# Late chunks transposed by DMA, five chunks loaded ahead of the first weights, and blocks of two chunks first, in a fused retention and FFN kernel

## The chip, the cores and the metric

One core of one Trainium2 chip. The metric is the device time of one execution in microseconds (us), the median of several runs; executions of one kernel mostly lie within 0.5% of their median. "Span" is the time between the first and the last instruction of the profiled execution; here a run is about 2 us longer than its span. A run counts as slow when it is over 1.5% above the fastest of its kernel; comparisons use fast runs.

## The reference

A linear attention with decay ("retention") over 4 batches, 8 heads, 768 steps and 64 dimensions, then an FFN with a squared ReLU over the 3072 tokens.

```python
for t in range(S):                                   # S = 768, per batch and head
    state = gamma * state + outer(k[t], v[t])
    y[t] = scale * q[t] @ state
x = y.transpose(0, 2, 1, 3).reshape(3072, 512)
out = square(relu(x @ w_in)) @ w_out                 # w_in 512 x 2048, w_out 2048 x 512
```

## The kernel before

The 3072 tokens are 24 chunks of 128. A chunk is loaded (q, k, v, 256 KB each), cast to bf16, q and k are transposed, one "visit" on TensorE does its attention (from the middle of the kernel on, one visit joins the end of a chunk's attention with the scores of the next), and its 128 rows `xt` go through FFN1 (by blocks of chunks) and FFN2 (by chunk).

The kernel does not write its instructions one after another. It records operations with their dependences and estimated durations, and a list scheduler in the kernel (`Plan`) simulates them and fixes the order on every engine before anything runs:

```python
def schedule(self, nbanks, max_open):
    ...
    while done < n:                       # the operation that can start first, by its estimates
        ...
                    key = (t, o["prio"], i)
                    if best is None or key < best[0]:
                        best = (key, i, eng)
        ...
            if move:                      # a DMA: charged to the shared DMA engines
                dur, n_desc = (dur[:2] if t < 50 else dur[:1] * 2), dur[2]
                eng_free[eng] = t + 0.08
                for w in range(2):
                    shared[w] = max(shared[w], t + self.DMA_LATENCY) + dur[w]
                end[i] = max(shared) + self.LAND
        ...
    return sorted(range(n), key=lambda i: (start[i], i))

SMALL = (1.20, 1.55, 65)                  # a 256 KB load: us of DMA, us of DMA, descriptors
PAIR = (1.4, 1.6, 9)
WIDE = (2.75, 2.75, 33)                   # a weight part, 1 MB
STORE = (0.72, 0.72, 9)
BLOCKS = [1, 1, 2, 2, 2, 4, 4, 4, 4]      # chunks per FFN1 block
ORDER = "p0 i0 i1 p1 i2 i3 o0 o1 o2 p2 o3"   # p: two chunks, i: w_in part, o: w_out part
```

From chunk 6 on the transposes are 32 small matmuls (from chunk 7 on inside the visit). They write the same PSUM tile `yy` that the visit uses, and ScalarE evicts them:

```python
def flips(m):
    ...
                    for a in range(2):
                        nc.tensor.transpose(tpv[...], bf[name][m % NBF][r, j, a, :], ident[r, r])   # 64x64

def evacuate(m):
    pl.add(f"E{m}", "ACT", 1.0, ("yy0", "yy1"), qkeys(m), ...)

def visit(m, n, t=None):                  # values and state of chunk m, scores and sums of n, transposes of t
    ...
```

## Time and profile before

| | |
|---|---|
| time | 226.85 us median of 3 runs (226.68 to 227.45) |
| span | 225.5 us |
| TensorE busy | 204.8 us (91%) |
| FFN matmuls alone, dense | 166 us: 192 groups of four 512-column matmuls at 0.865 us, read from the chain of waits |

The first lines are the groups of the page of before: source line, engine, operation, output<-inputs, shapes, count, then busy us and mean ns of one, then the idle time of the engine just before such instructions and what ended most of it.

```profile
L593 PE MATMUL fps<-xt,w_in 128*128 128x512 bf16 (+2 forms) x566 | 93.7, 309 | 3.9 <-POOL w_in L345 2.0
L631 PE MATMUL fps<-w_out,h 128*128 128x512 bf16 x368 | 90.1, 379 | 1.7 <-issue 1.3
...
L555 DVE TENSOR_TENSOR xt<-yy,yf 128x512 bf16<-128x512 f32 x24 | 16.6, 690 | 21.6 <-ACT qkT L436 18.1
L436 ACT ACTIVATE qkT<-yy 128x1024 bf16<-128x1024 bf16 x18 | 18.4, 1023 | 18.2 <-PE yy L468 17.5
```

L593 is FFN1 and L631 FFN2. The record lacks 26 of their 960 matmuls. The xt multiplication waits 18.1 us in all for the eviction of the transposes, which reads the same tile `yy`.

One piece of the chain of waits of before (start us, us, what) shows the cost of the transposes:

```profile
89.30 0.38 PE yy L389 x32
...
90.32 1.03 ACT qkT L436
...
91.37 0.70 DVE xt L555
...
92.12 1.89 PE fps L593 x8
```

The 32 small transposes take 0.38 us of TensorE, and FFN1 of a new block waits for their eviction and then for xt.

### The profile page before, as it was taken

How to read it: one execution, taken by the hardware profiler on the slowest of the kernel's cores; microseconds unless marked ns; L12 is line 12 of the kernel's file. 1: busy time of each engine (PE TensorE's matmuls, PEld its weight loads, DVE VectorE, ACT ScalarE, POOL GpSimd, SP SyncE). 2: the span in 40 equal slices, each digit the busy share in tenths (PEclk: the TensorE clock that was granted, in tenths of full speed). 3: DMA queues.
4: the chain of work that ended last, by engine and by line, in shares of the span. 5: the costliest groups of instructions: out<-in, count | busy, mean ns of one | idle time of the engine just before them, and what ended most of it. 6: DMA issues, size and time to landing. Idle time of an engine off the chain costs nothing.

```text
span 225.5 us, 7244 instructions
## 1 busy us (share of the span) xinstructions
PE 204.8 (91%) x3210; PEld 116.0 (51%) x3236; DVE 112.7 (50%) x250; ACT 106.0 (47%) x168; POOL 39.0 (17%) x65
## 2 busy tenths in 40 slices
PE   4786778699999999999989999999999999999993
PEld 1545667554577875455545554444444444444441
DVE  1583955873188786699957765432222222220000
ACT  8315635644357552677555555434335444343121
POOL 3213224224323322332242200000000000000000
PEclk9997999999999999999999999999999999999999
DMA  6999999999999999998988510110011110111212
GB/s 150 265 337 189 337 376 237 184 346 197 283 211 200 236 187 213 231 202 179 206 188 177 146 49 3 47 49 12 35 47 47 49 47 1 47 49 47 93 49 91
DMA packets 70975, 34.02 MB, mean 151 GB/s; under 512 B 63008, under 2 KB 63008, under 8 KB 70944
## 3 DMA queue, kind: packets, MB, share of 16 engines
q1 hardware_dynamic: 70944, 33.56, 58.8%
q8 instruction: 25, 0.41, 0.8%
q14 instruction: 6, 0.05, 0.1%
HBM read 27.26 MB, written 6.29 MB: 149 GB/s over the span
## 4 chain that ended last, share of the span: by engine, by line
PE 75%; SPq 11%; DMA 7%; issue 2%; ACT 2%; DVE 1%; POOL 0%; ACTq 0%; POOLq 0%
PE fps L631 34%; PE fps L593 32%; DMA qn<-in_q_dram 7%; SPq L569 6%; SPq L362 4%; PE yy L389 3%; PE yy L468 2%; SPq L356 2%; PE yy L453 1%; ACT qkT L436 1%; PE sc L479 1%; PE sc L490 1%; DVE xt L555 1%; POOL qs L345 0%; PE yy L402 0%
## 5 line engine op out<-in xcount | busy, mean ns | idle before, releaser
L593 PE MATMUL fps<-xt,w_in 128*128 128x512 bf16 (+2 forms) x566 | 93.7, 309 | 3.9 <-POOL w_in L345 2.0
L631 PE MATMUL fps<-w_out,h 128*128 128x512 bf16 x368 | 90.1, 379 | 1.7 <-issue 1.3
L598 ACT ACTIVATE h<-fps 128x512 bf16<-128x512 f32 x96 | 56.6, 596 | 52.6 <-PE fps L593 51.5
L593 PEld LDWEIGHTS <-w_in 128*128 128x128 bf16 x576 | 50.5, 99 | 35.4 <-issue 2.1
L603 DVE TENSOR_TENSOR h<-h 128x512 bf16<-128x512 bf16 x96 | 42.4, 456 | 49.7 <-ACT h L598 49.5
L631 PEld LDWEIGHTS <-h 128*128 128x128 bf16 x384 | 36.7, 98 | 42.9
L555 DVE TENSOR_TENSOR xt<-yy,yf 128x512 bf16<-128x512 f32 x24 | 16.6, 690 | 21.6 <-ACT qkT L436 18.1
L436 ACT ACTIVATE qkT<-yy 128x1024 bf16<-128x1024 bf16 x18 | 18.4, 1023 | 18.2 <-PE yy L468 17.5
L639 ACT ACTIVATE osb<-fps 128x512 f32<-128x512 f32 x24 | 14.3, 597 | 21.7 <-PE fps L631 21.4
L377 DVE TENSOR_TENSOR vs<-vn,vf 128x512 bf16<-128x512 f32 x24 | 17.6, 735 | 4.8 <-DMA vn<-in_v_dram 4.8
L345 POOL CAST ks<-kn 128x512 bf16<-128x512 f32 x20 | 13.5, 677 | 35.0 <-DMA kn<-in_k_dram 19.8
L345 POOL CAST qs<-qn 128x512 bf16<-128x512 f32 x21 | 14.7, 701 | 27.3 <-DMA qn<-in_q_dram 27.3
L546 DVE TENSOR_TENSOR state<-sc,state 128x256 bf16<-128x256 f32 x40 | 16.7, 419 | 0.5
L533 DVE TENSOR_TENSOR pt<-sc,cmask 128x512 bf16<-128x512 f32 x24 | 16.3, 681 | 0.0
L468 PE MATMUL yy<-qkT,state 64*64 64x64 bf16 x352 | 12.5, 198 | 1.0 <-issue 0.6
L453 PE MATMUL yy<-pt,vs 64*64 64x64 bf16 x384 | 7.8, 195 | 2.8 <-DVE pt L533 1.4
L468 PEld LDWEIGHTS <-state 64*64 64x64 bf16 x352 | 7.6, 105 | 2.0 <-PE yy L468 1.1
L453 PEld LDWEIGHTS <-vs 64*64 64x64 bf16 x384 | 5.3, 107 | 5.5 <-issue 2.9
L479 PE MATMUL sc<-qkT 64*64 64x64 bf16 x384 | 7.9, 196 | 0.1
L341 ACT ACTIVATE w_in<-wst 128x512 bf16<-128x512 f32 x7 | 4.1, 623 | 7.7 <-DMA wst<-in_moe_w_in_dram 7.6
L490 PE MATMUL sc<-vs,ks 64*64 64x64 bf16 x352 | 7.6, 196 | 0.0
L693 PE MATMUL fps<-ident 128*128 128x512 bf16 x12 | 5.8, 605 | 1.6 <-POOL ident L297 1.6
(45 smaller groups left out, 85.0 us busy)
## 6 DMA issues: line engine op xcount, KB each, us to landing
vn<-in_v_dram SPq DMA_DIRECT2D x24, 256.0 KB, 5.9
out_dram<-osb SPq DMA_DIRECT2D x24, 256.0 KB, 2.0
kn<-in_k_dram SPq DMA_DIRECT2D x18, 256.0 KB, 5.5
qn<-in_q_dram SPq DMA_DIRECT2D x18, 256.0 KB, 5.7
wst<-in_moe_w_in_dram SPq DMA_DIRECT2D x4, 1024.0 KB, 9.7
wst<-in_moe_w_out_dram SPq DMA_DIRECT2D x4, 1024.0 KB, 10.5
kn<-in_k_dram SPq DMA_DIRECT2D x3, 512.0 KB, 11.6
qn<-in_q_dram SPq DMA_DIRECT2D x3, 512.0 KB, 13.4
```

The costliest lines, as they stand in the source:

```text
L345: nc.gpsimd.tensor_copy(o, t)
L377: lambda: nc.vector.tensor_tensor(out=o[:], in0=t.rearrange("s (h d) -> s h d", h=H), in1=vf[:, i, :, None].to_broadcast([P, H, D]), op=AL ...
L436: lambda: nc.scalar.activation(qkT.rearrange("p x j (s t) -> p s (x j) t", s=2), tpv.rearrange("p s (g t) -> p s g t", t=L), AF.Copy), pri ...
L453: nc.tensor.matmul(yy[L * c : L * c + L, sub, p * L : p * L + L], lhsT=vs[r, 4 * a + j, :], rhs=pt[r, a, j, :], start=(p == 0), stop=True, ...
L468: nc.tensor.matmul(yy[L * c : L * c + L, sub, p * L : p * L + L], lhsT=st[r, j, :], rhs=qkT[r, 1, j, sub * L : sub * L + L], start=False, ...
L533: lambda: nc.vector.tensor_tensor(out=pt[:], in0=sc[:, :, 0:256].rearrange("s g (p t) -> s g p t", p=NJ), in1=cmask[:, None, None, :].to_b ...
L546: f = lambda cc=cc, j1=j1, j0=j0: nc.vector.tensor_tensor(out=sts[j1][:], in0=cc, in1=sts[j0][:], op=ALU.add)
L555: lambda: nc.vector.tensor_tensor(out=xt[:, :, u * C : u * C + C].rearrange("s p (g t) -> s g p t", g=2), in0=yy[:, :, 0:256].rearrange("s ...
L593: nc.tensor.matmul(ps[:, u * n : u * n + n], lhsT=w_in_bf[j][:, cb, c * P : (c + 1) * P], rhs=xt[:, cb, cols], start=(cb == 0), stop=(cb = ...
L598: nc.scalar.activation(h2[:, f0 : f0 + per, cols], ps[:].rearrange("p (u n) -> p u n", u=per), AF.Relu)
L603: nc.vector.tensor_mul(hv, hv, hv)
L631: nc.tensor.matmul(ps[:], lhsT=h2[:, fb, u * C : u * C + C], rhs=w_out_bf[j][:, c, :], start=(fb == 0), stop=(fb == NFB - 1))
```

## The change

The intent: take the late transposes off TensorE and ScalarE and give them to the DMA queue; load five chunks before the first weights, with neighbours in the queue from different chunks because the scheduler is told that this makes a load cheaper (0.95 us, not 1.20 to 1.55); begin with blocks of two chunks; and store the last chunk in two halves.

```diff
-SMALL = (1.20, 1.55, 65)
-PAIR = (1.4, 1.6, 9)
+SMALL = (0.95, 0.98, 65)          # neighbour from another chunk
+CLASH = (1.20, 1.55, 65)          # neighbour from the same chunk
+TURN = (1.05, 1.05, 9, 1.2)       # DMA transpose; the 4th number: us that it holds its queue
-BLOCKS = [1, 1, 2, 2, 2, 4, 4, 4, 4]
-SPLIT = 6
+BLOCKS = [2, 2, 2, 2, 4, 4, 4, 4]
+SPLIT = 8
+AHEAD = 4
-LEAD = 7
-NFP = 3
-F2LAG = 5.0
+LEAD = 5
+NPE = 7
+F2LAG = 6.0
-ORDER = "p0 i0 i1 p1 i2 i3 o0 o1 o2 p2 o3"
+ORDER = ("q0 q1 k0 k1 o0 v0 v1 q2 q3 k2 o1 q4 v2 k3 k4 k5 v3 o2 i0 i1 v4 q5 i2 i3 v5 q6 v6 o3 k6 k7 v7 q7")
 ...
     def transpose(m):
-        pl.add(f"T{m}", "PE", 0.45, ..., lambda: flips(m), ...)      # 32 of 64x64
-        evacuate(m)
+        if m >= NPE:
+            pl.add(f"X{m}", "SP", TURN, (bfk, bfq), qkeys(m),
+                   lambda: nc.sync.dma_start_transpose(out=..., in_=...), prio=-0.5)
+            return
+        for x, name in enumerate("kq"):                              # 4 of 128x128 each, evicted by ACT or DVE
 ...
+            parts = 2 if q4 == NM - 1 else 1                         # the last chunk's output in halves
```

(Cut: the buffers, the removed paired loads, the plumbing of `AHEAD`, and a change of the scheduler itself: it now charges every DMA with holding its queue, 0.6 us unless a fourth number says otherwise, where it charged 0.08. The comments and the shortened arguments are mine.)

More of the change, by code (lines that the diff above doesn't have):

```diff
@@ L38, in __init__, with add @@
         self.readers = {}
-    def add(self, name, eng, dur, reads=(), writes=(), fn=None, prio=0.0, lat=0.0, bank=None, after=(), count=0):
+    def add(self, name, eng, dur, reads=(), writes=(), fn=None, prio=0.0, lat=0.0, bank=None, after=(), count=0, tag=None):
         i = len(self.ops)
@@ L60, in add @@
         self.ops.append(dict(i=i, name=name, eng=eng, flex=flex, deps=sorted(deps), fn=fn,
-                             prio=prio, lat=lat, bank=bank, count=count))
+                             prio=prio, lat=lat, bank=bank, count=count, tag=tag))
         return i
@@ L87, in schedule @@
         outstanding = {e: [] for e in eng_free}
+        recent = []
         done = 0
@@ L121, in schedule @@
                     t = max(t, out_.pop(0)[0])
+                hold = dur[3] if len(dur) > 3 else 0.6
             start[i] = t
@@ L130, in schedule @@
             if move:
-                dur, n_desc = (dur[:2] if t < 50 else dur[:1] * 2), dur[2]
-                eng_free[eng] = t + 0.08
+                n_desc = dur[2]
+                if dur is SMALL:
+                    if recent[-1:] == [o["tag"]]:
+                        dur = CLASH
+                recent.append(o["tag"])
+                dur = dur[:2] if t < 50 else dur[:1] * 2
+                eng_free[eng] = t + hold
                 for w in range(2):
@@ L136, in schedule @@
                 out_.append((max(shared), n_desc))
-                dur = 0.08
+                dur = hold
             else:
@@ L194 @@
 WPRIO = {"in": -2.0, "out": 2.0}
-ORDER = "p0 i0 i1 p1 i2 i3 o0 o1 o2 p2 o3"
+ORDER = (
+    "q0 q1 k0 k1 o0 v0 v1 q2 q3 k2 o1 q4 v2 k3 k4 k5 v3 o2 i0 i1 v4 q5 i2 i3 v5 q6 v6 o3 k6 k7 v7 q7"
+)
 def dma_order(nm):
-    seq = []
-    for t in ORDER.split() + [f"c{m}" for m in range(nm)]:
-        n = int(t[1:])
-        if t[0] == "p":
-            new = [("k", 2 * n), ("q", 2 * n), ("v", 2 * n), ("v", 2 * n + 1)]
-        else:
-            new = [(x, n) for x in "kqv"] if t[0] == "c" else [("in" if t[0] == "i" else "out", n)]
-        seq += [x for x in new if x not in seq]
-    return seq
+    names = {"i": "in", "o": "out"}
+    seq = [(names.get(t[0], t[0]), int(t[1:])) for t in ORDER.split()]
+    return seq + [(x, m) for m in range(nm) for x in "kqv" if (x, m) not in seq]
 @with_exitstack
@@ L246 @@
         assert 512 % (n * C) == 0 and x // 4 == (x + n - 1) // 4
-    NLD, NBF, NQT, NXT, NH2, NWS, NOSB, NST = 4, 4, 4, 4, 3, 4, 3, 6
+    NLD, NBF, NQT, NXT, NH2, NWS, NOSB, NST = 4, 5, 5, 4, 3, 4, 3, 6
     NBANK = 4
@@ L265 @@
     ld = {x: sb(f"{x}n", [P, NLD, H * D], FP32) for x in "qkv"}
-    bf = {x: [sb(f"{x}s{j}", [P, NJ, 2, D] if x != "v" else [P, H, D], BF16) for j in range(NBF)] for x in "qkv"}
+    kq = [sb(f"kqs{j}", [P, 2, NJ, 2, D], BF16) for j in range(NBF)]
+    bf = {"k": [t[:, 0] for t in kq], "q": [t[:, 1] for t in kq]}
+    bf["v"] = [sb(f"vs{j}", [P, H, D], BF16) for j in range(NBF)]
     qkts = [sb(f"qkT{j}", [P, 2, NJ, P], BF16) for j in range(NQT)]
@@ L278 @@
     yy = psum.tile([P, 2, 512], FP32, name="yy")
-    tpv = yy[:, :, 256:512].bitcast(BF16)
     fps = [psum.tile([P, 512], FP32, name=f"fps{j}") for j in range(NBANK)]
@@ L352, in prepare @@
             t = ld[x][:, slot, :]
-            if x != "v" and m < 2 * NFP:
-                if m % 2 == 0:
-                    pl.add(f"ld{x}{m}", "SP", PAIR, (), (f"ld{x}{slot}", f"ld{x}{slot + 1}"),
-                           lambda x=x: nc.sync.dma_start(
-                               ld[x][:, slot : slot + 2, :].rearrange("s u n -> s (u n)"),
-                               src[x][b, :, i * C : (i + 2) * C, :].rearrange("h (w t) d -> w h (t d)", t=16)),
-                           prio=dma_prio[(x, m)])
-                continue
             pl.add(f"ld{x}{m}", "SP", SMALL, (), (f"ld{x}{slot}",),
@@ L364, in prepare @@
                        src[x][b, :, i * C : (i + 1) * C, :].rearrange("h s d -> s h d")),
-                   prio=dma_prio[(x, m)])
+                   prio=dma_prio[(x, m)], tag=m)
         for x in "kq":
             t, o = ld[x][:, slot, :], bf[x][m % NBF]
-            if m < 2 * NFP:
-                pl.add(f"c{x}{m}", CAST[x], 0, (f"ld{x}{slot}",), (f"bf{x}{m % NBF}",),
-                       lambda on, t=t, o=o: copy_on(on, o.rearrange("s j a d -> s (j a d)"), t), prio=urgency(m))
-                continue
             pl.add(f"c{x}{m}", CAST[x], 0, (f"ld{x}{slot}",), (f"bf{x}{m % NBF}",),
@@ L380, in prepare @@
                prio=urgency(m))
-    def flips(m):
-        for x, name in enumerate("kq"):
-            for j in range(NJ):
-                for sub in range(2):
-                    r = slice(L * sub, L * sub + L)
-                    for a in range(2):
-                        nc.tensor.transpose(tpv[L * a : L * a + L, sub, 256 * x + j * L : 256 * x + j * L + L],
-                                            bf[name][m % NBF][r, j, a, :], ident[r, r])
-    def flip_rows(m, x):
-        to, key = (sc, "sc") if x == "k" else (yy, "yy")
-        for u in range(2):
-            bt = bf[x][(m + u) % NBF].rearrange("s j a d -> s (j a d)")
-            def fn(u=u, bt=bt):
-                for t in range(8):
-                    for a in range(2):
-                        nc.tensor.matmul(to[L * a : L * a + L, u, L * t : L * t + L], lhsT=bt[:, t * D : t * D + D],
-                                         rhs=ident.rearrange("p (w h) -> p w h", h=H)[:, :, NJ * a : NJ * a + NJ],
-                                         start=True, stop=True, skip_group_check=True)
-            pl.add(f"T{x}{m}.{u}", "PE", 0.35, (f"bf{x}{(m + u) % NBF}", "ident"), (f"{key}{u}",), fn,
-                   prio=-200 + m, lat=0.2, count=16)
-        cols = to.rearrange("p s n -> p (s n)").rearrange("p (t u w j) -> p u j w t", u=2, j=NJ, w=8)
-        for u in range(2):
-            o = qkts[(m + u) % NQT][:, "kq".index(x)].rearrange("p j (w t) -> p j w t", t=16)
-            pl.add(f"E{x}{m + u}", EVAC, 0, (f"{key}0", f"{key}1"), (f"qkT{(m + u) % NQT}.{x}",),
-                   lambda on, u=u, o=o: copy_on(on, o, cols[:, u]), prio=urgency(m + u), lat=0.05)
@@ L413, in natural_keys @@
-    def natural_keys(m):
-        qkT, ks = qkts[m % NQT], bf["k"][m % NBF]
-        o1 = {}
-        def back():
-            ps = fps[o1["op"]["bank_index"]].bitcast(BF16)
-            for j in range(NJ):
-                nc.tensor.transpose(ps[:, j * P : j * P + P], qkT[:, 0, j, :], ident[:])
-        i0 = pl.add(f"B{m}", "PE", 0.24, (qkeys(m)[0], "ident"), (f"gB{m}",), back, prio=-200 + m, lat=0.2, count=4,
-                    bank=("open", ("B", m), False))
-        o1["op"] = pl.ops[i0]
-        pl.add(f"G{m}", EVAC, 0, (f"gB{m}",), (f"bfk{m % NBF}",),
-               lambda on: copy_on(on, ks.rearrange("s j a d -> s (j a d)"),
-                                  fps[o1["op"]["bank_index"]].bitcast(BF16)[:, 0:512]),
-               prio=urgency(m), bank=("close", ("B", m)))
@@ L430, in qkeys, with fn @@
     def qkeys(m):
         return [f"qkT{m % NQT}.{x}" for x in "kq"]
-    def evacuate(m):
-        qkT = qkts[m % NQT]
-        pl.add(f"E{m}", "ACT", 1.0, ("yy0", "yy1"), qkeys(m),
-               lambda: nc.scalar.activation(
-                   qkT.rearrange("p x j (s t) -> p s (x j) t", s=2),
-                   tpv.rearrange("p s (g t) -> p s g t", t=L), AF.Copy), prio=urgency(m), lat=0.05)
-    def transpose(m):
-        pl.add(f"T{m}", "PE", 0.45, (f"bfk{m % NBF}", f"bfq{m % NBF}", "ident"), ("yy0", "yy1"),
-               lambda: flips(m), prio=-200 + m, lat=0.2, count=32)
-        evacuate(m)
+    def transpose(m):
+        qkT, t = qkts[m % NQT], kq[m % NBF]
+        if m >= NPE:
+            pl.add(f"X{m}", "SP", TURN, (f"bfk{m % NBF}", f"bfq{m % NBF}"), qkeys(m),
+                   lambda: nc.sync.dma_start_transpose(out=qkT.rearrange("p x j t -> p (x j) t"),
+                                                       in_=t.rearrange("s x j a d -> s (x j a d)")), prio=-0.5)
+            return
+        for x, name in enumerate("kq"):
+            o1 = {}
+            def fn(x=x, o1=o1):
+                ps = fps[o1["op"]["bank_index"]].bitcast(BF16)
+                for j in range(NJ):
+                    nc.tensor.transpose(ps[:, j * P : j * P + P], t[:, x, j].rearrange("s a d -> s (a d)"), ident[:])
+            i0 = pl.add(f"T{name}{m}", "PE", 0.26, (f"bf{name}{m % NBF}", "ident"), (f"gT{name}{m}",), fn,
+                        prio=-200 + m, lat=0.2, count=4, bank=("open", ("T", m, x), False))
+            o1["op"] = pl.ops[i0]
+            pl.add(f"E{name}{m}", EVAC, 0, (f"gT{name}{m}",), (qkeys(m)[x],),
+                   lambda on, x=x, o1=o1: copy_on(on, qkT[:, x].rearrange("p j t -> p (j t)"),
+                                                  fps[o1["op"]["bank_index"]].bitcast(BF16)[:, 0:512]),
+                   prio=urgency(m), lat=0.05, bank=("close", ("T", m, x)))
@@ L492, in sums, with visit @@
                                      start=False, stop=True, skip_group_check=True)
-    def visit(m, n, t=None):
+    def visit(m, n):
         reads, writes = [], []
-        if t is not None:
-            reads += [f"bfk{t % NBF}", f"bfq{t % NBF}", "ident"]
-            writes += ["yy0", "yy1"]
         if m is not None:
@@ L508, in fn @@
         def fn():
-            if t is not None:
-                flips(t)
             if m is not None:
@@ L521, in fn @@
                 apply(m, 1)
-        dur = 0.19 + (0.26 if m is not None else 0) + (0.26 if n is not None else 0) + (0.26 if t is not None else 0)
+        dur = 0.19 + (0.26 if m is not None else 0) + (0.26 if n is not None else 0)
         if n is None:
@@ L526, in visit @@
                prio=-300 + n if m is None else -300 + m if m < PACE else (m - LEAD) * 8, lat=0.25,
-               count=32 * ((m is not None) + (n is not None) + (t is not None)) + 1)
-        if t is not None:
-            evacuate(t)
+               count=32 * ((m is not None) + (n is not None)) + 1)
         if n is not None:
@@ L620, in ffn2 @@
             h2 = h2s[g % NH2]
-            grp = ("f2", q4)
-            o1 = {}
             slot = q4 % NOSB
-            for j in range(4):
-                reads = [f"h{g % NH2}.{u}.{4 * j + c}" for c in range(4)] + [f"wout{j}.{c}" for c in range(4)]
-                def mm(j=j, o1=o1, h2=h2, u=u):
-                    ps = fps[o1["op"]["bank_index"]]
-                    for c in range(4):
-                        fb = 4 * j + c
-                        nc.tensor.matmul(ps[:], lhsT=h2[:, fb, u * C : u * C + C], rhs=w_out_bf[j][:, c, :],
-                                         start=(fb == 0), stop=(fb == NFB - 1))
-                i0 = pl.add(f"F2.{q4}.{j}", "PE", 0.866, reads, (f"g{grp}",), mm,
-                            prio=(q4 + F2LAG) * 8 + 2 * j + 1, lat=0.2,
-                            bank=("open", grp, True) if j == 0 else ("use", grp), count=4)
-                if j == 0:
-                    o1["op"] = pl.ops[i0]
@@ L638, in ffn2 @@
-            pl.add(f"O{q4}", "ACT", 0.6, (f"g{grp}",), (f"osb{slot}",),
-                   lambda o1=o1, slot=slot: nc.scalar.activation(
-                       osbs[slot][:], fps[o1["op"]["bank_index"]][:], AF.Copy),
-                   prio=q4, bank=("close", grp))
-            pl.add(f"st{q4}", "SP", STORE, (f"osb{slot}",), (),
-                   lambda q4=q4, slot=slot: nc.sync.dma_start(out[rows(q4) : rows(q4) + C, :], osbs[slot][:]), prio=-1)
+            parts = 2 if q4 == NM - 1 else 1
@@ new lines, in ffn2, with mm @@
+            w = DM // parts
+            for part in range(parts):
+                ns = slice(part * w, part * w + w)
+                grp = ("f2", q4, part)
+                keys = [f"osb{slot}.{part}"] if parts > 1 else [f"osb{slot}.0", f"osb{slot}.1"]
+                o1 = {}
+                for j in range(4):
+                    reads = [f"h{g % NH2}.{u}.{4 * j + c}" for c in range(4)] + [f"wout{j}.{c}" for c in range(4)]
+                    def mm(j=j, o1=o1, h2=h2, u=u, ns=ns, w=w):
+                        ps = fps[o1["op"]["bank_index"]]
+                        for c in range(4):
+                            fb = 4 * j + c
+                            nc.tensor.matmul(ps[:, 0:w], lhsT=h2[:, fb, u * C : u * C + C], rhs=w_out_bf[j][:, c, ns],
+                                             start=(fb == 0), stop=(fb == NFB - 1))
+                    i0 = pl.add(f"F2.{q4}.{j}" + f"/{part}" * (parts > 1), "PE", 0.866 / parts, reads, (f"g{grp}",), mm,
+                                prio=(q4 + F2LAG) * 8 + 2 * j + 1 + part * 0.5, lat=0.2,
+                                bank=("open", grp, True) if j == 0 else ("use", grp), count=4)
+                    if j == 0:
+                        o1["op"] = pl.ops[i0]
+                pl.add(f"O{q4}" + f"/{part}" * (parts > 1), "ACT", 0.2 + 0.4 / parts, (f"g{grp}",), keys,
+                       lambda o1=o1, slot=slot, ns=ns, w=w: nc.scalar.activation(
+                           osbs[slot][:, ns], fps[o1["op"]["bank_index"]][:, 0:w], AF.Copy),
+                       prio=q4, bank=("close", grp))
+                pl.add(f"st{q4}" + f"/{part}" * (parts > 1), "SP", STORE, keys, (),
+                       lambda q4=q4, slot=slot, ns=ns: nc.sync.dma_start(out[rows(q4) : rows(q4) + C, ns], osbs[slot][:, ns]),
+                       prio=-1)
@@ L653 @@
         n = m + 1
-        early = n < 2 * NFP and n % 2 == 0
-        if early:
-            prepare(n)
-            prepare(n + 1)
-            flip_rows(n, "k")
-        elif 2 * NFP <= n <= SPLIT:
-            prepare(n)
+        for x in range(0 if m < 0 else m + AHEAD, min(NM, m + AHEAD + 1)):
+            prepare(x)
+            transpose(x)
         if n < NM and n < SPLIT:
@@ L663 @@
                 visit(m, None)
-            if early:
-                flip_rows(n, "q")
-                natural_keys(n)
-                natural_keys(n + 1)
-            elif n >= 2 * NFP:
-                transpose(n)
             visit(None, n)
         else:
-            if n == SPLIT:
-                transpose(n)
-            t = n + 1 if n + 1 < NM else None
-            if t is not None:
-                prepare(t)
-            visit(m if m >= 0 else None, n if n < NM else None, t)
+            visit(m, n if n < NM else None)
         while done < NB and blk0[done] + blocks[done] - 1 == m:
```

## The prediction

> **What bounds the kernel now.** From about 50 us on, TensorE: the busy table by ten-microsecond stretches shows it at 9.1 to 9.95 us of 10. Before that it has 5.9 to 8.2, while the DMA share is about 1.0. So there are two stages: a start limited by loads, then dense matmuls. In the chain of waits four 512-column matmuls take 0.865 us; the FFN (24 chunks x 2 x 16 x 512 columns) needs 192 x 0.865 = 166 us. By 46.8 us (timeline of TensorE) only four chunks have their first FFN product (13.8 us of dense work); about 28 us of the start are lost. Later about 5 us are lost, mostly where FFN1 waits for the transpose eviction (1.03 us on ScalarE) and then xt (0.70 us).
>
> **What the change does.**
> 1. Transposes. 18 chunks are transposed inside the visit by 32 64x64 matmuls (0.38 us each in the chain, 3% of the span) and evicted in 1.02 us by ScalarE. Now chunks 7 to 23 go by DMA transposes of 256 KB; chunks 0 to 6 take eight 128x128 transposes and two evictions. That removes 17 x 0.3 to 0.38 = 5 to 6.5 us of TensorE and most eviction waits (3 to 4 us). Cost: DMA time. The Trainium skill, "DMA: Bandwidth & Descriptors", section "Latency and other measured facts", gives 261 GB/s for a DMA transpose, so an estimated 1.0 us each; no run shows it yet. Per chunk the DMA has 3 loads of 1.25 to 1.4 us, a transpose and a 0.7 us store, about 6 us, against 7.5 us of TensorE: hidden.
> 2. Load order. Five chunks' k and q and four chunks' v come ahead of the first weights. In before FFN1 starts at 14.8 us but starves (gaps of 2 us, 2.6 us). Now it should start at 20 to 24 us: 14 loads of 256 KB at 1.0 to 1.3 us, then 2.75 us for w_in. From there two blocks share each weight part (3.5 us of matmuls per 2.75 to 3.7 us of DMA), so TensorE is nearly dense from about 22 us. Before's trace shows no clear difference between neighbours of the same and of different chunks (1.34, 1.42, 1.35 us per load), so I half believe it.
> 3. Blocks of two first: 256-column matmuls, same columns, small gain.
> 4. The last chunk in halves: the tail (3.7 us after the last matmul) shortens by 0.3 to 0.5 us.
>
> **Sum.** FFN start 21.5 + FFN 166 + 20 visits x 0.68 = 13.6 + transposes of chunks 5 and 6, 1 + remaining idle 4.5 + tail 3.4 = 210 us span; a run is 1.4 us above its span: **211.5 us**, 8 in 10 within **206 to 218**. Faster by over 2%: 0.93; within 2%: 0.05; slower: 0.02.
>
> **What would show it.** First FFN1 matmul at 20 to 24 us; FFN2 before 40 us; TensorE over 9 of 10 from 25 us; the 64x64 transposes gone from the chain; DMA transposes landing within 3 to 6 us, no matmul waiting for one; loads under 1.1 us apiece at the start if the order matters.
>
> **What would make it wrong.** Loads at 1.4 us as before (FFN start 25 us, 215 us in all); DMA transposes much slower than copies, or holding up SyncE's queue so that visits wait (218 us or more); TensorE's clock lowered during the thin start (0.60 from 20 to 24 us in before); weights starving FFN1 between 22 and 45 us. Better if loads reach 0.95 us and TensorE never waits (206 us).

## More of the kernel before

The next lines are busy times by stretch of before. After the length come, engine by engine, the busy us and the number of instructions, then the granted clock of TensorE as a share, the DMA share and GB/s.

```profile
0.00:60.00 60.00, 46.48 (x918) 31.77 (x923) 34.13 (x84) 29.67 (x50) 18.13 (x34) 0.97 1.00 263
60.00:150.00 90.00, 86.94 (x1991) 51.91 (x1995) 64.41 (x133) 50.11 (x74) 20.86 (x31) 1.00 0.71 161
150.00:226.00 76.00, 71.36 (x325) 32.30 (x331) 14.20 (x33) 26.27 (x44) 0.00 (x0) 0.99 0.13 49
```

There are three stages. Up to 60 us the loads limit everything. From 60 to 150 us visits and FFN alternate and TensorE is idle for only 3 us. From 150 us the FFN runs alone.

## The result, and the profile after

**233.06 us median of 4 runs (231.98 to 233.32), slower by 2.7%**: the ratio is 1.0269, interval 1.0223 to 1.0316. Ratios here are the mean time of one kernel's fast runs over that of before's fast runs of the same rounds, so not quite the ratio of the medians that are quoted.

The same stretches, of after:

```profile
0.00:60.00 60.00, 48.40 (x705) 33.36 (x706) 38.42 (x93) 29.86 (x50) 20.67 (x38) 1.00 1.07 261
60.00:150.00 90.00, 79.96 (x1293) 41.66 (x1294) 57.30 (x116) 29.86 (x51) 18.77 (x31) 0.98 1.25 210
150.00:230.00 80.00, 76.65 (x452) 36.23 (x451) 17.36 (x39) 27.04 (x46) 0.00 (x0) 1.00 0.13 49
```

Between 60 and 150 us TensorE has far fewer instructions, as intended, but is idle for 10.0 us (it was 3.1). Nearly all of it has one name. This is TensorE's list of waits in just that stretch of after (engine, line, waited for: us in total, times, longest):

```profile
PE sc L436 <- DMA qkT<-kqs: 10.0, 9, 1.7
```

L436 are the scores, the part of a visit that needs the next chunk, and `qkT<-kqs` is the DMA transpose. The timeline of TensorE shows two such places and what they bring on (start us, us, instruction, count, idle before):

```profile
102.98 0.23 PE L425 MATMUL yy<-qkT,state 64*64 64x64 bf16 x8
104.27 0.32 PE L436 MATMUL sc<-qkT 64*64 64x64 bf16 x16 [1.06 <-DMA qkT<-kqs]
...
110.37 0.32 PE L436 MATMUL sc<-qkT 64*64 64x64 bf16 x16 [1.72 <-DMA qkT<-kqs]
...
110.82 4.45 PE L543 MATMUL fps<-xt,w_in 128*128 128x512 bf16 x12
115.10 1.03 PE L586 MATMUL fps<-w_out,h 128*128 128x512 bf16 x4
```

The stretch around the second place, in the form of the tables by stretch above:

```profile
110.00:120.00 10.00, 9.63 (x136) 4.45 (x137) 6.98 (x14) 2.26 (x4) 2.46 (x4) 0.83 1.27 225
```

Twelve matmuls of 512 columns take 4.4 us in the chain of waits, 0.37 us each, where 0.216 is normal. The stretch 110 to 120 us has a granted clock of 0.83: for 3.4 us TensorE ran at half speed just after the 1.72 us wait, and 1.7 us were lost. The Trainium skill, "TensorE: Matmul & The Clock Gate", Part 1 ("The HAM clock gate"), says that the clock drops to half after an idle window of about 3.4 us and is full again after a busy window of the same length. The 3.4 us of the slow piece agree with the second; with the first the trace does not, for the longest single wait was 1.72 us. The other eight waits for transposes, of 0.2 to 1.4 us, had no slow piece after them; why this one had is not shown.

The groups of after that answer to those of before:

```profile
L543 PE MATMUL fps<-xt,w_in 128*128 128x256 bf16 (+1 forms) x512 | 96.7, 335 | 2.3 <-POOL w_in L351 1.8
L586 PE MATMUL fps<-w_out,h 128*128 128x512 bf16 (+1 forms) x400 | 92.0, 371 | 0.0
...
L505 DVE TENSOR_TENSOR xt<-yy,yf 128x512 bf16<-128x512 f32 x24 | 16.5, 688 | 8.5 <-PE yy L425 8.4
...
L436 PE MATMUL sc<-qkT 64*64 64x64 bf16 x384 | 8.0, 204 | 10.0 <-DMA qkT<-kqs 10.0
```

The eviction waits did go (xt no longer waits for ScalarE, and the 64x64 transposes are gone). They were replaced by the wait for the DMA transposes. The odd thing is that there was FFN work to do meanwhile: when the last wait for a transpose ended, at 149.4 us, some 75 us of FFN were still to come. TensorE took its instructions in the order of its list: at 110.82 us twelve FFN matmuls ran right behind the awaited visit, with no wait of their own. So a visit whose transpose has not landed holds up the FFN matmuls behind it.

The start gave nearly nothing. FFN1 began at 26.2 us (before: 14.8), and by 60 us both kernels had done about the same FFN work: 26.2 us of dense matmuls after, 25.1 before. (These are the matmuls of the record by their columns at 0.422 ns each, which is 0.865 us over 2048 columns; three that the record of before lacks are filled in.)

### The profile page after: what moved, and what is told of

Its sections match the earlier page's. It is cut to its first block, busy times and chain, and to the rows that moved or that the text cites. A ratio compares the mean times of both kernels' runs of the same rounds, so it can differ in the third digit from the quotient of the medians.

```text
span 230.0 us, 5691 instructions
## 1 busy us (share of the span) xinstructions
PE 205.0 (89%) x2448; PEld 111.3 (48%) x2448; DVE 113.1 (49%) x248; ACT 86.7 (38%) x146; POOL 39.4 (17%) x68
## 4 chain that ended last, share of the span: by engine, by line
PE 46%; DMA 31%; SPq 14%; DVE 3%; POOL 2%; ACT 1%; issue 1%; POOLq 0%; ACTq 0%
PE fps L586 27%; PE fps L543 17%; DMA qkT<-kqs 11%; SPq L360 8%; DMA qn<-in_q_dram 5%; DMA kn<-in_k_dram 5%; DMA wst<-in_moe_w_out_dram 4%; DMA wst<-in_moe_w_in_dram 4%; SPq L519 3%; SPq L384 2%; DMA vn<-in_v_dram 2%; POOL kqs L351 1%; PE sc L436 1%; DVE vs L371 1%; ACT h L548 1%
## 5 line engine op out<-in xcount | busy, mean ns | idle before, releaser
L543 PE MATMUL fps<-xt,w_in 128*128 128x256 bf16 (+1 forms) x512 | 96.7, 335 | 2.3 <-POOL w_in L351 1.8
L586 PE MATMUL fps<-w_out,h 128*128 128x512 bf16 (+1 forms) x400 | 92.0, 371 | 0.0
L586 PEld LDWEIGHTS <-h 128*128 128x128 bf16 x400 | 38.1, 98 | 40.8 <-issue 0.5
L594 ACT ACTIVATE osb<-fps 128x512 f32<-128x512 f32 (+1 forms) x25 | 14.5, 580 | 41.5 <-PE fps L586 41.5
L351 POOL CAST kqs<-kn 128x512 bf16<-128x512 f32 x24 | 14.9, 622 | 62.2 <-DMA kn<-in_k_dram 50.3
L351 POOL CAST kqs<-qn 128x512 bf16<-128x512 f32 x23 | 14.3, 624 | 21.0 <-DMA qn<-in_q_dram 21.0
L436 PE MATMUL sc<-qkT 64*64 64x64 bf16 x384 | 8.0, 204 | 10.0 <-DMA qkT<-kqs 10.0
L393 PE MATMUL fps<-ident,kqs 128*128 128x128 bf16 x56 | 7.9, 289 | 6.1 <-POOL kqs L351 6.1
L436 PEld LDWEIGHTS <-qkT 64*64 64x64 bf16 x384 | 5.5, 115 | 12.5 <-DMA qkT<-kqs 11.0
L347 ACT ACTIVATE qkT<-fps 128x512 bf16<-128x512 bf16 x9 | 5.4, 597 | 13.6 <-PE fps L393 13.5
L393 PEld LDWEIGHTS <-kqs 128*128 128x128 bf16 x56 | 4.5, 124 | 10.2 <-POOL kqs L351 9.8
```

The costliest lines, as they stand in the source:

```text
L351: nc.gpsimd.tensor_copy(o, t)
L436: nc.tensor.matmul(sc[cs, a, j * L : j * L + L], lhsT=qkT[r, 0, j, cs], rhs=qkT[r, 1, j, cs], start=(j == 0), stop=True, skip_group_check= ...
L543: nc.tensor.matmul(ps[:, u * n : u * n + n], lhsT=w_in_bf[j][:, cb, c * P : (c + 1) * P], rhs=xt[:, cb, cols], start=(cb == 0), stop=(cb = ...
L586: nc.tensor.matmul(ps[:, 0:w], lhsT=h2[:, fb, u * C : u * C + C], rhs=w_out_bf[j][:, c, ns], start=(fb == 0), stop=(fb == NFB - 1))
```

## The experiments

**Theories.** (A) *Order*: the scheduler is told too low costs of transfers, so it places visits in TensorE's list before their data can have landed. (B) *Capacity*: 17 transposes more are too much for the DMA engines, and no order helps. (C) *Queue*: a transpose holds SyncE's queue for 1.3 to 3.6 us, so the loads behind it start late. (D) *Start*: five chunks ahead of the weights is what costs.

### 1. The disputed costs by themselves

A kernel of transfers alone (wrong output, one run), with fences between the stages: 12 loads in the order k, q, v of one chunk; 12 with neighbours of different chunks; 12 DMA transposes; 12 loads with a transpose after every third; 24 stores.

> A kernel of transfers alone (its output is zeros, wrong on purpose): 12 loads with k, q, v of one chunk after one another, 12 with neighbours of different chunks, 12 DMA transposes alone, 12 loads with a transpose after every third, 24 stores; a fence between the stages. If the plan of the changed kernel is right, loads come at 1.2 to 1.5 us with neighbours of one chunk and at 0.95 to 0.98 us with different ones, a transpose costs 1.05 us of the DMA engines and 1.2 us of the issuing queue, and the mixed group of three loads and one transpose takes about 4.0 to 5 us. If the transposes are what the kernel lost to, a transpose alone costs 2 us or more, and the issuing queue is held 2.3 us. If neighbours do not matter, both load stages come at 1.2 us.

Landings are seen as waits of VectorE, which touches each tile in turn. A selection from the timeline of VectorE (start us, us, instruction, idle before), first from the two load stages, then from the transposes:

```profile
15.86 0.06 DVE L39 MEMSET ld<- 128x2 f32 x1 [1.14 <-DMA ld<-in_q_dram]
...
19.55 0.06 DVE L39 MEMSET ld<- 128x2 f32 x1 [1.14 <-DMA ld<-in_k_dram]
20.76 0.06 DVE L39 MEMSET ld<- 128x2 f32 x1 [1.16 <-DMA ld<-in_v_dram]
21.97 0.06 DVE L39 MEMSET ld<- 128x2 f32 x1 [1.14 <-DMA ld<-in_q_dram]
...
39.50 0.06 DVE L41 MEMSET qkT<- 128x1 uint32 x1 [1.39 <-DMA qkT<-kqs]
40.84 0.06 DVE L41 MEMSET qkT<- 128x1 uint32 x1 [1.28 <-DMA qkT<-kqs]
42.19 0.06 DVE L41 MEMSET qkT<- 128x1 uint32 x1 [1.29 <-DMA qkT<-kqs]
```

The first of these lines lies in the stage with neighbours of one chunk; 19.55 to 21.97 us are in the stage with different ones. In the DMA packets' ends both stages show 1.20 us per load. So the cheap 0.95 us load does not exist: **1.20 us with either neighbour**.

A transpose alone comes every 1.38 us (35.25 to 50.47 us: 11 steps) and holds the queue for 1.28 us. That pace is about the queue's own: with some 0.1 us between them the issues follow one another just as fast, and each transpose lands 3.3 us after its issue, the last like the first, so no backlog of transfers grew. The mixed group of three loads and a transpose has a pitch of 4.66 us (52.05 to 66.03 us: three steps), and there the queue is held longer (timeline of SyncE's queue):

```profile
52.85 0.57 SPq L29 DMA_DIRECT2D ld<-in_k_dram  x1
53.47 0.57 SPq L29 DMA_DIRECT2D ld<-in_q_dram  x1
54.09 0.79 SPq L29 DMA_DIRECT2D ld<-in_v_dram  x1
54.98 2.04 SPq L33 DMA_TRANSPOSE qkT<-kqs  x1
```

Beyond what three loads cost (3.60 us) a transpose among loads adds about 1.06 us. So two of the scheduler's new numbers were too low: 0.95 for a load against 1.20, and 1.2 of queue for a transpose against 1.28 alone and about 2 between loads. Its 1.05 of DMA for a transpose was below the 1.38 of transposes alone, but it is what a transpose adds among loads.

### 2. No DMA transposes

```diff
-NPE = 7
+NPE = 24
```

> The changed kernel with every chunk transposed on TensorE in 128x128 pieces (no DMA transposes), all else as changed. If the late DMA transposes cost the dense stage its gain: the 10 us of waits for them and the 1.7 us of half clock go, 17 x 0.3 us of transposes come back, so 220 to 226 us. If the load order at the start is what lost the time, it stays at 230 us or goes up by the 5 us of transposes.

Measured: 233.81 us (ratio 1.0346, interval 1.0292 to 1.04), no faster. Its waits of TensorE:

```profile
PE fps L393 <- POOL kqs L351: 11.8, 15, 1.9
PE fps L543 <- POOL w_in L351: 2.1, 1, 2.1
```

I had expected 220 to 226 us if the transposes were the culprit, and they were not. With them gone, the wait moved one step up: the transposes on TensorE (L393) now wait 11.8 us for the cast of q and k, that is, for the loads. It looks like the same early placing, with another piece of data that is late. This speaks against B and for A, but a late load fits D as well, which is still open.

### 3. The same kernel with higher numbers in its scheduler

```diff
-SMALL = (0.95, 0.98, 65)
-TURN = (1.05, 1.05, 9, 1.2)
+SMALL = (1.20, 1.20, 65)
+TURN = (2.0, 2.0, 9, 2.3)
```

> The changed kernel, but the scheduler that fixes the order of the instructions is told 1.20 us per load (was 0.95), 2.0 us of DMA and 2.3 us of queue per transpose (were 1.05 and 1.2). Only the order changes. If TensorE lost time because its order placed the visits before their transposes had landed, the waits of TensorE for DMA transposes (10 us in all) fall under 3 us and the time is 212 to 222 us. If the DMA engines' capacity is the bound, no order helps: 228 us or more.

Measured: **219.74 us, ratio 0.9736 (0.9676 to 0.9796)**: 2.6% faster than before, with the same operations, bytes and number of DMA transposes as the 233 us kernel. What differs is the order (and eight more filler matmuls, and eight casts and evictions of the start that the scheduler gave to other engines, by the built program). The 60 to 150 us stretch of this run, and TensorE's only wait in it:

```profile
60.00:150.00 90.00, 89.13 (x1289) 46.15 (x1288) 56.46 (x117) 33.58 (x57) 21.02 (x30) 1.00 1.16 211
```

```profile
PE fps L543 <- DVE xt L505: 0.8, 1, 0.8
```

TensorE is busy for 89.1 of 90 us (79.96 in after). The wait for DMA transposes is gone, although they come no sooner. These are the transposes of after and of real_cost (hold of the queue in ns, minimum, median and maximum; first and last start in us):

```profile
L384 SPq DMA_TRANSPOSE qkT<-kqs x17: 1296/2321/3617, 59.5 to 146.7; - x17
L384 SPq DMA_TRANSPOSE qkT<-kqs x17: 1232/2206/3050, 58.2 to 149.7; - x17
```

One comes every 5.45 us in after and every 5.72 in real_cost (16 steps each), and they land after 4.9 and 4.7 us (median). What changed is what TensorE did meanwhile: by 150 us it had done 91 us of FFN in after and 104 in real_cost. Theory B falls: the transfers can be hidden. Theory C loses ground too, for each transpose still holds SyncE's queue for 2.2 us. The run was before those costs were known; its 2.0 us is above what a transpose costs alone (1.38), which the runs below take apart.

TensorE's list is not the only order that changed. These are the waits of SyncE's queue for the casts that a transpose needs, from 60 to 150 us, in after and in real_cost:

```profile
SPq L384 <- POOL kqs L351: 22.5, 11, 3.0
SPq L384 <- POOL kqs L351: 4.7, 4, 1.8
```

So in after the transposes stood too early in SyncE's queue as well. One scheduler makes both orders, and no run here changes one without the other.

### 4. The transposes from another queue

```diff
-pl.add(f"X{m}", "SP", TURN, ... nc.sync.dma_start_transpose(
+pl.add(f"X{m}", "ACT", TURN, ... nc.scalar.dma_start_transpose(
```

> The changed kernel with the 17 DMA transposes issued from ScalarE's queue in place of SyncE's. If a transpose holds its issuing queue for 2.3 us and the loads behind it are thereby late, loads now go on meanwhile: the pitch of chunks in the middle falls from 5.5 us to 4.5 us and TensorE's waits shrink to under 5 us, 222 to 227 us, unless ScalarE's evictions suffer (each holds back FFN1 banks). If the DMA engines are the limit, the pitch stays 5.5 us and the time 230 us or more.

Measured: 231.45 us (ratio 1.0243, interval 1.019 to 1.0296), the same as after within the intervals. From the first to the last transpose the pitch per chunk is 5.52 us (57.1 to 145.5 us in 16 steps), against 5.45 in after (59.5 to 146.7). Freeing SyncE's queue did not let the chunks come faster. The time alone would not decide, for TensorE's waits changed:

```profile
PE fps L543 <- ACT h L548: 5.5, 3, 2.5
PE sc L436 <- DMA qkT<-kqs: 4.7, 4, 1.9
```

The waits for transposes fell from 10.0 to 4.7 us, as theory C would have it, and 5.5 us of waits for ScalarE's evictions came in their place, the exception that I had named. Still, with the pitch unchanged here, and the queue held as long in real_cost at 219.74 us, theory C has no support. What does pace the chunks stays open. Between the first and the last transpose of after stand 44 loads and 8 stores (by its trace); at 1.20 us a load, 1.06 a transpose and about 0.7 a store (stores alone in the first experiment) that is an estimated 75 us of the 87.

### 5. One number at a time

```diff
-SMALL = (0.95, 0.98, 65)                # load_cost, both_cost
+SMALL = (1.20, 1.20, 65)
-TURN = (1.05, 1.05, 9, 1.2)             # turn_cost, both_cost
+TURN = (1.4, 1.4, 9, 2.0)
```

Only the load's number:

> The changed kernel with one number of its scheduler corrected: a load costs 1.20 us (measured alone: 1.20 us with either kind of neighbour), not 0.95. The number for a transpose stays too low. If the wrong cost of the loads is what placed the visits too early, nearly all of the gain of the run with both numbers raised comes back: 217 to 222 us, TensorE waits for transposes under 3 us. If the wrong cost of the transposes did it, 226 us or more.

Only the transpose's numbers:

> The changed kernel with only the transpose's numbers corrected: 1.4 us of DMA and 2.0 us of the queue (measured alone 1.37 and 1.28 us, 2.05 us of queue between loads); loads stay at 0.95 us. If the loads' number is to blame it stays at 229 to 233 us; if the transposes' number is, 217 to 223 us.

Both at what was measured:

> Both numbers at the values measured alone (1.20; 1.4 and 2.0). Expected 216 to 220 us, as good as or a little better than the run with the transposes overstated at 2.0 and 2.3 us, since no visit is held back longer than needed. If margin is what helps and not truth, it is slower than that run.

Measured: 226.15 us for the three fast runs (226.33 with a slow one; ratio 0.9982, interval 0.9919 to 1.0045), 225.37 (0.995, 0.9893 to 1.0007) and 221.23 (0.9775, 0.9716 to 0.9834), the last a little above the 216 to 220 expected. I had expected one of the two numbers to bring back nearly all; each brings a little over half (6.9 and 7.7 of 11.8 us). The reason shows in the order itself. The built program tells how much FFN work stands before the visit of each chunk in TensorE's list (counted in groups of four 512-column matmuls, 0.865 us each). Between the visits of chunks 8 and 18 that is, per chunk:

| kernel | load; transpose; queue, as the scheduler is told | FFN per chunk, us | plus a visit of 0.67 us | TensorE's waits for DMA transposes (PE line of the waits) | time, us |
|---|---|---|---|---|---|
| after | 0.95; 1.05; 1.2 | 4.06 | 4.73 | 10.0 us | 233.06 |
| load_cost | 1.20; 1.05; 1.2 | 4.50 | 5.17 | 7.0 us (this profile slow) | 226.15 |
| turn_cost | 0.95; 1.4; 2.0 | 4.50 | 5.17 | 4.0 us | 225.37 |
| both_cost | 1.20; 1.4; 2.0 | 4.93 | 5.60 | 0.8 us | 221.23 |
| real_cost | 1.20; 2.0; 2.3 | 5.19 | 5.86 | none | 219.74 |

A chunk arrives every 5.45 us (the pitch of the transposes in after). Where TensorE's list asks for one every 4.73 or 5.17 us, TensorE waits; from 5.60 us on it does not. A list that asks for chunks too early pays with idle TensorE; one that asks late pays nothing here, for there is FFN work to fill with. The waits of SyncE's queue for casts (60 to 150 us) fall down the table in the same way: 22.5, 18.6, 17.2, 13.6 and 4.7 us. Whether overstating the transpose (real_cost) is truly better than the measured number (both_cost) stays open: 0.9736 against 0.9775, from different rounds, with overlapping intervals.

### 6. The worth of the DMA transposes under a better order

```diff
-SMALL = (0.95, 0.98, 65)
-NPE = 7
+SMALL = (1.20, 1.20, 65)
+NPE = 24
```

> Loads at 1.20 us in the scheduler and all chunks transposed on TensorE: what the DMA transposes are worth under a truthful order. 17 x 0.3 us of TensorE and their evictions: 5 to 8 us slower than the run with only the load's number corrected, 224 to 229 us. If the DMA transposes are worth nothing, equal to it.

Measured: 230.22 us (ratio 1.0161, interval 1.0101 to 1.0222), against 226.15 for load_cost in the same rounds: the DMA transposes are worth 4.1 us there (I had expected 5 to 8), and 9.0 us against both_cost, where their cost is raised too. This run still waits 6.6 us for casts before its transposes on TensorE; I did not decompose it further.

### 7. The wrong number in the old kernel

```diff
 # the kernel before, no other edit
-SMALL = (1.20, 1.55, 65)
+SMALL = (0.95, 0.98, 65)
```

> The kernel before with one number of its scheduler lowered to the changed kernel's: a 256 KB load at 0.95 us instead of 1.20 (1.55). Only the order changes. If too low a cost of transfers harms by itself, whatever else is in the kernel, this is 2 to 8 us slower than before. If the DMA transposes are needed for the harm, it stays within 1 us of before.

Measured: 234.77 us, **ratio 1.0394 (1.0331 to 1.0457)**: 3.9% slower than the same kernel with its own number. No DMA transpose is involved. So the optimistic load cost harms by itself, and by more than the whole change lost (2.7%). In this program 25.9 us of FFN stand before the visit of chunk 8, where before has 33.7. But that its visits come too early is not shown to be how it loses the time: by 60 us it had done 21.2 us of FFN against 25.1 in before, with seven visits begun in each, so about half of the 8 us was lost in the start, and after 60 us no wait of its TensorE is longer than 1.8 us.

### 8. The start

Two chunks ahead of the weights, as before the change, with the numbers of real_cost:

```diff
-ORDER = ("q0 q1 k0 k1 o0 v0 v1 q2 q3 k2 o1 q4 v2 k3 k4 k5 v3 o2 i0 i1 v4 ...")
+ORDER = ("q0 k0 v0 q1 k1 v1 i0 i1 q2 k2 v2 i2 i3 q3 k3 v3 o0 o1 q4 k4 v4 o2 o3 ...")
```

> The same raised numbers, but only two chunks loaded ahead of the first weights, as before, and neighbours of one chunk. If loading five chunks ahead is a gain of its own, this is slower than 219.7 us by 3 us or more though FFN1 starts at 18 to 20 us instead of 26.6. If the order of the start is neutral (all kernels had done some 26 us of FFN by 60 us), it is within 2 us of it.

Measured: 220.91 us (ratio 0.9802, interval 0.9725 to 0.988), against 0.9736 (0.9676 to 0.9796) for real_cost. FFN1 starts at 15.9 us instead of 26.7, yet by 60 us the FFN work done is 26.8 us against 26.6. This order of the start is neutral within what these runs can tell (with the raised numbers; with those of after it was not tried), and theory D falls with it: five chunks ahead neither lost the time nor won any.

Fillers for the clock, with the numbers of real_cost:

```diff
-WARM = 20.0
-FILL = 0.8
+WARM = 27.0
+FILL = 1.0
```

> The run with the scheduler's numbers raised (1.20 us; 2.0 and 2.3 us) plus nine more filler matmuls up to 27 us instead of 20. In every run of the changed start so far TensorE's full clock is granted for good only from 28 to 32 us, in before from 23 us. If fillers bring the full clock to the first FFN matmuls (26.6 us), 4 us at half speed become full: 1.5 to 2 us faster than that run, ratio to before 0.965. If the clock does not follow fillers, no change: 0.973.

Measured: 218.87 us (ratio 0.9689, interval 0.9623 to 0.9756). The full clock did come earlier (granted 1.00 from 28 to 32 us, where real_cost has 0.67), but the gain of about 0.5% is inside the intervals: inconclusive.

A better order, found by trying orders of the early transfers in the scheduler with the numbers of real_cost, and eight chunks on TensorE:

```diff
-NPE = 7
-ORDER = ("q0 q1 k0 k1 o0 v0 v1 q2 q3 k2 o1 q4 v2 k3 k4 k5 v3 o2 i0 i1 v4 q5 i2 i3 v5 q6 v6 o3 k6 k7 v7 q7")
+NPE = 8
+ORDER = ("v1 k0 q2 q0 k1 v0 q1 o1 v3 k2 o2 q3 v2 k3 k4 k5 o0 i0 q4 i1 v4 q5 i2 i3 v5 k6 v7 o3 q6 q7 v6 k7")
```

> The same raised numbers with another order of the early transfers (found by trying orders against the scheduler with truthful numbers) and eight chunks on TensorE instead of seven. Expected 1 to 4 us faster than 219.7 us: ratio to before 0.955 to 0.97. If the start is neutral, 0.973.

Measured: **217.52 us, ratio 0.9615 (0.9563 to 0.9666)**: the best, 3.9% faster than before. By 60 us it had done 28.5 us of FFN (26.6 in real_cost), and TensorE is busy for all of 100 to 150 us. Two things were changed at once, so the gain over real_cost (other rounds, intervals just apart) is not split between them.

## Why the prediction was wrong

The predicted time was 211.5 us (206 to 218); it is 233.06. The form of the sum holds, so the failed terms can be named, with what the profile of after has in their place:

| term | predicted, us | measured in after, us |
|---|---|---|
| FFN start | 21.5 | 26.2 |
| FFN, dense | 166 | 166 (0.865 us per group) |
| 20 visits | 13.6 | 13.4 (0.67 each) |
| transposes of chunks 5 and 6 | 1 | about 1 |
| **remaining idle** | **4.5** | **19.8** (what is left of the span of 230.0) |
| tail | 3.4 | 3.6 |

- **The step that failed** is the line under "Transposes": "Per chunk the DMA has ... about 6 us, against 7.5 us of TensorE: hidden", and with it "no matmul waiting for one" and the 4.5 us of remaining idle. The comparison of rates is right over the whole kernel, and real_cost shows that the transfers can be hidden. But being hidden also needs an order that lets them be. TensorE's list does not alternate one visit with one chunk's whole FFN: it ran the visits ahead, one per 4.73 us, against 5.45 us for the data. Of the 19.8 us, 10.0 are waits for DMA transposes and 1.7 the half clock after one of them. About 1.9 more went where the FFN began at a low speed (from 26.24 us 40 matmuls of 256 columns took 6.21 us; at half of 0.216 us each it would be 4.3), which the prediction had among its risks. The remainder of about 6 us I did not split up.
- **The FFN start** was off by 4.7 us, and not by the cost of a load: I had put it at 1.0 to 1.3 us, and it is 1.20. The sum of the start left things out. In after 15 loads, not 14, come before the first weights; the first lands at 3.9 us and the last at 21.9; the first w_in part lands 3.4 us later (2.75 predicted), and its casts follow, from 25.3 to 26.5 us. "FFN start 25 us" among the risks was nearer in number, but for another reason (loads at 1.4 us). And the consequence was wrong too: two_ahead starts its FFN1 11 us earlier than real_cost and is no faster. By 60 us all of these starts had done 26 to 27 us of FFN, whenever the first FFN matmul ran.
- **Right**: the 64x64 transposes leave the chain, the eviction waits go (18.1 us of VectorE idling for ScalarE), the DMA transposes land within 3.6 to 6.4 us, and the transfers fit beside TensorE in principle.
- **A transpose's cost** was put at 1.0 us from the 261 GB/s of the Trainium skill, "DMA: Bandwidth & Descriptors", "Latency and other measured facts". Alone one came every 1.38 us for 256 KB (190 GB/s), at about the pace of its queue, and among loads it added about 1.06 us, so this term was about right. What the scheduler had too low was the load and the hold of the queue.
- **The tail** did not shorten (3.6 us from the last matmul to the end, 3.7 before): the last chunk's two half evictions still follow one another at the end.
- The risk "holding up SyncE's queue so that visits wait (218 us or more)" named the symptom, but in turn_act, which took the transposes off that queue, neither the pitch nor the time changed, and in real_cost the waits went with the queue as it was.

The deeper fault was one of method. The diff carries the scheduler's belief about the hardware: lower load costs stand in it in plain sight. I asked whether the belief was true, saw that the trace of before did not support it, and then counted only its direct effect (a later start). I did not ask what a *false* belief does to the order of everything after it. Experiment 7 shows that it alone costs the old kernel 3.9%.

What stays open: the split of the remaining idle time of after; what paces the chunks at 5.45 us; how much is due to the order on TensorE and how much to that on SyncE's queue; why load_cost and turn_cost, with equal demand per chunk, have waits of 7.0 and 4.0 us (one profile was slow); and whether margin beyond the measured cost of a transpose helps.

## What to carry to other kernels

A scheduler that fixes the order in advance turns its cost estimates into instruction order, so an estimate that is too low turns into waits on the engine that executes in order, even where work and bandwidth abound. Measure each transfer in the mix in which it occurs before writing its cost down. Where other work can fill the time, a cost that is too high did no harm that could be measured here (real_cost against both_cost). When reading a diff, treat changed cost numbers as a change of the program: compare the rate at which the in-order list *asks* for data (here 4.73 us per chunk) with the rate at which it *arrives* (5.45 us), not only the totals.

## What the Trainium skill lacked or had wrong

- "DMA: Bandwidth & Descriptors", "Latency and other measured facts": 261 GB/s for a DMA transpose with a non-contiguous middle dimension, about 350 to 400 for a contiguous one, without its size or direction. From SBUF to SBUF, 128 partitions by 1024 bf16, contiguous in each partition, it was 190 GB/s here when transposes followed one another alone (1.38 us per 256 KB, at about the pace of one issuing queue), and an estimated 247 GB/s from the 1.06 us that one adds among loads. The 350 to 400 was not reached.
- No page that I found gives how long a DMA transpose of this size holds its issuing queue on this chip: 1.28 us alone, about 2.0 us between loads, up to 3.6 us in after, against 0.5 to 0.6 us for a load issued when there is room.
- No page that I found says whether neighbouring loads of different tensors at the same offset slow one another. They do not here: 1.20 us per 256 KB load in runs of 256 B either way; a 256 KB store in runs of 2 KB took about 0.7 us.
- "TensorE: Matmul & The Clock Gate", Part 1: half clock after an idle window of about 3.4 us. In after a half-clock piece of 3.4 us followed a single wait of 1.72 us, and waits of up to 1.42 us had none after them. The same Part tells of half clock after many short idles in another kernel, but gives no length for them.
